# Other step durations for the list scheduler of an attention and two feed-forward layers

## The chip, the cores and the metric

The kernel runs on one core of a Trainium2 chip, in a single launch. The metric is the device time of that core in microseconds (us). Before the change it is 1063.86 us, the median of three runs.

## The reference

Four batches of eight heads, 576 positions, head size 64, go through a causal softmax attention that is mixed with a linear "memory" read; the result is a matrix of 2304 tokens by 512, which passes two feed-forward layers with 2048 hidden columns each.

```python
scores = scale * np.matmul(q, k.transpose(0, 1, 3, 2))        # causal mask, softmax -> a
local = np.matmul(a, v)
q_p = phi(q)                                                  # phi(x) = x + 1 for x > 0, exp(x) otherwise
mem_out = einsum('bhsd,bhde->bhse', q_p, M_prev) / (einsum('bhsd,bhd->bhs', q_p, z_prev) + 1e-06)
attn = g * mem_out + (1 - g) * local                          # g: one gate for each head
x = attn as (2304, 512)
r = np.maximum(x @ w_in1, 0); y = (s * r * r + b) @ w_out1    # first layer
h = y @ w_in2; out = (h * tanh(softplus(h))) @ w_out2         # second layer
```

All of it is float32. The feed-forward products are kept exact enough by splitting each operand into a high and a low part and adding three products.

## The kernel before

**An order made at build time.** Every operation is entered with `add(engine, us, prio, f, reads, writes)` as a step: an engine (PE, ACT, DVE, POOL, or the DMA queue that SyncE issues), a duration in microseconds that the program believes, and a rank. `Plan.order` then plays all steps through on a model of the engines: whenever an engine of the model is free, it takes the step of lowest rank among those whose inputs the model has ready and whose buffers (the `Ring`s, with few slots each) are free. The order in which the model starts the steps is the order in which the instructions are written into each engine's queue. On the chip each engine works its queue strictly in that order, and waits at its head where an input is late. So a duration written in `add` costs no time itself; it only decides what comes ahead of what. The model also has a TensorE clock of two levels (`pe_end`).

**Ranks.** Attention comes in units, one for a batch and a head. The eight of batch 0 are cut in two halves (ranks `PRE_A + STEP_A*h` and `PRE_B + STEP_B*h`); the 24 of batches 1 to 3 have `UNIT0 + UNIT*i`, that is 84.65, 106.78, 128.91 and so on. The first layer's weights are converted in 32 pieces of 128 x 512 (`convert`), whose ranks grow by `CONV` (3.0, 3.81, 4.18, 3.12 for a piece of the four groups), from 0 to 109.8. The first layer's products rank from 206 up by 5.53 a step, behind everything they compete with on TensorE; their elementwise work has the rank -1, ahead of everything.

**A unit of attention.** POOL, ACT and DVE make phi of q (`ex`); `norm_phi` (L423 to L426) forms the dot of each row of phi with z, one instruction for a tile of 128 rows, with its sum into `nm`; two small DVE steps make the gated reciprocal. For each tile, PE makes scores, DVE masks them and takes the largest (L476), POOL writes phi times the reciprocal into the same tile (`Pt`, L488: "phi's product"), and ACT takes the exponential (L485). The rows are then scaled, transposed by PE (L531), evicted by ACT and DVE, multiplied by M and v (L559), and written to `x_d`.

**A piece of weights.** The weights come as 8-byte words and are made into float32 by six instructions: a DMA (L620) into `raw` (two slots, with four more of borrowed room early on), two on ACT (L627 and L632), two on DVE (L634 and L635), one on POOL (L637). For the first layer ACT then rounds to the high part (L644) and DVE takes the low part (L646). The intermediate `w` has two slots (`w32=2`). For the second layer the piece goes to DRAM instead (L649), and comes back later.

**The first layer.** For 16 blocks of hidden columns (`fc`), `mm_in` (L698) makes h by 12 matmuls, ACT and DVE square the positive part and split it (L741, L742, L744, L745), and `y_part` (L758) adds 12 more matmuls to the accumulators `accs[j]`, which lie in the PSUM banks y0 and y1 for the first blocks of tokens. Columns `fc` 12 to 15 need the last group of weight pieces.

**Fillers.** While the model's time is between 7 and 85 us, the model sees PE idle, and it has done little in this tick of the model's clock, it puts in `zero_product` (L932 to L935): a matmul of zeros of 256 columns into the tile `idle`, which takes the place of bank y1. It computes nothing that is used.

Of the kernel before, what the change touches and what calls it, by code (L numbers as in the profile page):

```python
# [13 lines left out]
U32 = mybir.dt.uint32  # L14
AF = mybir.ActivationFunctionType
ALU = mybir.AluOpType
# [6 lines left out]
SIGN = -0x80000000  # L23
PE, ACT, DVE, POOL, DMA = range(5)
# [93 lines left out]
class Plan:  # L118
# [29 lines left out]
    def add(self, engine, us, prio, f, r=(), w=(), after=(), keep=(), share=1.0):  # L148


        bufs = list({id(b): b for b in (*r, *w, *keep) if b.ring is not None}.values())
        new = [b for b in bufs if b.maker is None]
        waits = {id(s): s for b in r for s in b.writers}
        waits.update((id(s), s) for s in after)
        s = Step(engine, us, prio, f, list(waits.values()), bufs, new)
        s.share = share
        s.left = len(waits)
        for x in waits.values():
            x.next.append(s)
        for b in bufs:  # L160
            b.users += 1
            if b.maker is None:
                b.maker = s
            elif id(b.maker) not in waits:
                b.maker.next_start.append(s)
                s.left += 1
        for b in w:
            b.writers.append(s)
        self.steps.append(s)
        return s  # L170
# [100 lines left out]
def attention_then_two_ffn(ctx: ExitStack, tc: tile.TileContext, qk, qz, vm, beta,  # L271
# [3 lines left out]
    nc = tc.nc  # L275
    B, H = qk.shape[:2]
    NQ, D = qz.shape[3] - 1, qz.shape[4]
# [20 lines left out]
    add = plan.add  # L298
# [66 lines left out]
    def unit(b, h, prio, groups=(TA, TB), place=None):  # L365
# [4 lines left out]
        def add(engine, us, f, r=(), w=(), keep=(), share=1.0):  # L370
            attention_steps.append(plan.add(engine, us, prio, f, r, w, keep=keep, share=share))
# [8 lines left out]
        else:  # L380
            qk_b, qn_b, vx_b = Buf(R["qk"], [P, SP + S]), Buf(R["qn"], [P, (NQ + 1) * D]), Buf(R["vx"], [P, NQ * D])
# [5 lines left out]
        def qkt(a, n):  # L387

            return qk_b.t[:, a - q0_:a - q0_ + n]

        def kt(a, n):
            return qk_b.t[:, k0_ + a:k0_ + a + n]
# [22 lines left out]
        ex = Buf(R["ex"], [P, NQ, D])  # L415
        nm = Buf(R["nm"], [P, 16])
        lo_t, n_t = tiles[0], len(tiles)
# [10 lines left out]
        def norm_gate():  # L428
# [3 lines left out]
        add(ACT, act_us(n_t * D), lambda: nc.scalar.activation(ex.t[:, mine], ex.t[:, mine], AF.Exp), [ex], [ex])  # L432
        add(DVE, dve_us(n_t * D), lambda: nc.vector.scalar_tensor_tensor(ex.t[:, mine], q_rows(), 0.0, ex.t[:, mine],
                                                                         op0=ALU.max, op1=ALU.add), [ex, qn_b], [ex])
        add(DVE, 0.22 * n_t, norm_phi, [ex, qn_b], [nm, qn_b])
        add(DVE, 0.13, norm_gate, [nm], [nm])
        add(DVE, 0.09, lambda: nc.vector.reciprocal(nm.t[:, mine], nm.t[:, mine]), [nm], [nm])  # L437

# [1 line left out]
        if not early:  # L440
# [4 lines left out]
                                                                    op=ALU.subtract), [qk_b, A], [A])  # L445
            add(DVE, dve_us(nkc), lambda: nc.vector.tensor_tensor(B2.t[:, :nkc], kt(0, nkc), B1.t[:, :nkc].bitcast(F32),
                                                                    op=ALU.subtract), [qk_b, B1], [B2])
# [8 lines left out]
        Pt = {t: Buf(R[ring[t]], [P, size[t]]) for t in tiles}  # L456
# [3 lines left out]
        def score(t):  # L460
            w = D + P * t
            for i, (lo, hi) in enumerate([(0, w)] if w <= 512 else [(0, w // 2 + 32), (w // 2 + 32, w)]):
                ps = Buf(R["a"], [P, 512])

                def mm(lo=lo, hi=hi, ps=ps):
                    if early:
                        nc.tensor.matmul(ps.t[:, :hi - lo], qkt(t * P, P)[:D], kt(lo, hi - lo)[:D],  # L467
                                         start=True, stop=True)
                    else:
                        lhs = A.t[:, t * P - q0_:(t + 1) * P - q0_]  # L470
                        nc.tensor.matmul(ps.t[:, :hi - lo], lhs, B1.t[:, lo:hi], start=True, stop=False)
                        nc.tensor.matmul(ps.t[:, :hi - lo], lhs, B2.t[:, lo:hi], start=False, stop=True)

                def least(lo=lo, hi=hi, ps=ps, i=i):

                    nc.vector.tensor_tensor_reduce(Pt[t].t[:, D + lo:D + hi], ps.t[:, :hi - lo],  # L476
                                                   mask[:, SP - w + lo:SP - w + hi], -SCALE,
                                                   mx.t[:, t:t + 1] if i else HUGE, ALU.add, ALU.min,
                                                   mx.t[:, t + i:t + i + 1])

                add(PE, (hi - lo) * 0.0017 if early else 0.07 + (hi - lo) * 0.0008, mm, score_in, [ps], [Pt[t], mx, rs], 0.5 if early else 1.0)
                add(DVE, 0.14 + 0.00105 * (hi - lo), least, [ps] + [mx_in[t]] * i, [Pt[t], mx_in[t]], [mx])

            def exp():
                nc.scalar.activation(Pt[t].t[:, D:w + D], Pt[t].t[:, D:w + D], AF.Exp, bias=mx.t[:, t + i:t + i + 1],  # L485
                                     scale=-1.0, accum_out=rs.t[:, t:t + 1])

            add(POOL, 0.3, lambda: nc.gpsimd.tensor_scalar(Pt[t].t[:, :D], ex.t[:, t, :], nm.t[:, t:t + 1], 1.0,  # L488
                                                           op0=ALU.mult, op1=ALU.mult), [ex, nm], [Pt[t]])
            add(ACT, 0.28 + 0.00083 * w, exp, [Pt[t], mx_in[t]], [Pt[t], rs_in[t]], [mx, rs])  # L490

# [114 lines left out]
    def convert(layer, prio, which, r, j, raw, after=()):  # L606


        w_in, w_out = ((w_in1, w_out1), (w_in2, w_out2))[layer - 1]
        fc = r * FPR + j  # L610
        src = w_in[j * P:(j + 1) * P, r * 512:(r + 1) * 512] if which == "in" else w_out[fc * P:(fc + 1) * P, :]
        w = Buf(R["w32"], [P, 512], I32)

        def words():
            return raw.t[:, :1024].rearrange("p (n two) -> p n two", two=2)

        def f32():
            return w.t.bitcast(F32)

        add(DMA, 1.5, prio, lambda: nc.sync.dma_start(words(), src.bitcast(I32).rearrange("p (n two) -> p n two", two=2)),  # L620
            w=[raw], after=after).lag = 1.0 if layer == 1 else 3.0

        e = on((C_W if layer == 1 else C2_W)[j])
        add(e, 0.52 if e == ACT else 0.335, prio,
            (lambda: nc.scalar.activation(f32(), words()[:, :, 1].bitcast(F32), AF.Copy, scale=2.0 ** -112)) if e == ACT else  # L627
            (lambda: nc.vector.tensor_scalar(f32(), words()[:, :, 1].bitcast(F32), 2.0 ** -112, None, op0=ALU.mult)),
            [raw], [w])

        low_words = Buf()
        add(ACT, 0.52, prio, lambda: nc.scalar.activation(words()[:, :, 0], words()[:, :, 0].bitcast(U32), AF.Copy,  # L632
                                                          scale=2.0 ** -29), [raw], [low_words])
        add(DVE, 0.335, prio, lambda: nc.vector.tensor_scalar(w.t, w.t, 3, None, op0=ALU.logical_shift_left), [w], [w])  # L634
        add(DVE, 0.6, prio, lambda: nc.vector.scalar_tensor_tensor(w.t, words()[:, :, 1], SIGN, w.t,  # L635
                                                                   op0=ALU.bitwise_and, op1=ALU.bitwise_or), [raw, w], [w])
        add(POOL, 1.23, prio, lambda: nc.gpsimd.tensor_tensor(w.t, w.t, words()[:, :, 0], op=ALU.add),  # L637
            [raw, low_words, w], [w])
        if layer == 1:
            hi, lo = W[1, f"w{which[0]}h", r], W[1, f"w{which[0]}l", r]  # L640
            hi_dve, lo_dve = C_HI[j] == "D", C_LO[j] == "D"
            half = Buf()
            add(DVE if hi_dve else ACT, 0.335 if hi_dve else 0.52, prio,
                lambda: (nc.vector.tensor_copy if hi_dve else nc.scalar.copy)(hi.t[:, j, :], f32()), [w], [hi, half])  # L644
            add(DVE if lo_dve else POOL, 0.6 if lo_dve else 1.23, prio,
                lambda: (nc.vector if lo_dve else nc.gpsimd).tensor_tensor(lo.t[:, j, :], f32(), hi.t[:, j, :].bitcast(F32),  # L646
                                                                           op=ALU.subtract), [w, half], [lo])
        else:
            add(DMA, 0.75, prio, lambda: nc.sync.dma_start(W2D[which, r][:, j, :], f32()), [w], [w2_in[which, r]]).lag = 1.5  # L649
# [239 lines left out]
    accs, halves = {}, {}  # L889
# [21 lines left out]
    for r in range(NR):  # L911
        for which in ("in", "out"):
            for j in (0, 2):
                split_second(-0.5, which, r, j)

    seq = [(blk, fc) for blk in range(NB2) for fc in range(NFC)]
    for i in range(len(seq) + LAG2):
        if i < len(seq):
# [11 lines left out]
    idle = []  # L930

    def zero_product():  # L932
        if not idle:
            idle.append(ps_y.tile([P, 512], F32, tag="y1_0", name="idle"))
        nc.tensor.matmul(idle[0][:, :256], mask[:, :P], mask[:, :256], start=True, stop=True)  # L935
# [46 lines left out]
```

## Time and profile before

| | us |
|---|---|
| median of 3 runs (1062.65 to 1064.59) | 1063.86 |
| the profiled execution's own time | 1059.81 |
| its span, from the first to the last instruction | 1058.0 |
| PE (matmuls) busy | 1027.7 |
| DVE busy | 665.0 |
| ACT busy | 533.4 |
| POOL busy | 218.5 |

The profile is of one execution. An engine is busy while one of its instructions runs; overlapping instructions count once. On DVE and ACT the record of an instruction overlaps the next one's by some hundredths of a microsecond, so the time that an instruction takes of its engine is read from its start to the next start, where the two follow without a gap. PE's clock is given as a share of its full speed: 1.00 is 2.4 GHz and 0.50 is 1.2 GHz.

### The profile page before, as it was taken

Reading aid. Unit: us, or ns where it says so; the run is one execution under the profiler, and the core shown is the slowest. Engines: PE = TensorE matmul, PEld = TensorE weight load, DVE = VectorE, ACT = ScalarE, POOL = GpSimd, SP = SyncE. Lnnn points to the kernel's source line nnn. Section 1 sums busy time; section 2 is a strip of 40 time slices with the busy share of each in tenths; the row PEclk is TensorE's granted clock in tenths of the full one; section 3 lists DMA queues with packets and bytes.
Section 4 is the critical chain, followed back from the end, with each engine's and each line's share of the span. In section 5 each row is a group of like instructions: output and inputs, shape, how many; then the busy total and the mean of one; then the engine's idle time right before and its main releaser. Section 6 shows DMA issues by size and latency. Waiting matters only on the chain. (4 is left out here: it accounts for less than half of the span.)

```text
span 1058.0 us, 17549 instructions
## 1 busy us (share of the span) xinstructions
PE 1027.7 (97%) x6011; PEld 891.4 (84%) x6011; DVE 665.0 (63%) x1962; ACT 533.4 (50%) x1267; POOL 218.5 (21%) x337
## 2 busy tenths in 40 slices
PE   7999997999999999999989999999999999999998
PEld 4567887999999999998768888888888888888887
DVE  7899999999999999955986666422312322222122
ACT  6887896888778888855445554312110211111111
POOL 6753443332333332212233300000000000000000
PEclk9999999999999999999999999999999999999999
DMA  9654562334322422257456764200200100010010
GB/s 274 186 168 141 174 182 76 105 112 144 95 87 80 134 87 87 71 176 212 136 169 200 241 205 155 86 1 1 80 1 1 35 26 0 1 40 1 1 41 20
DMA packets 52073, 106.66 MB, mean 101 GB/s; under 512 B 6672, under 2 KB 27664, under 8 KB 51984
## 3 DMA queue, kind: packets, MB, share of 16 engines
q1 hardware_dynamic: 51552, 105.54, 32.0%
q8 instruction: 47, 0.77, 0.3%
q14 instruction: 42, 0.34, 0.1%
q10 hardware_dynamic: 432, 0.01, 0.0%
HBM read 82.97 MB, written 22.54 MB: 100 GB/s over the span
## 5 line engine op out<-in xcount | busy, mean ns | idle before, releaser
L831 ACT ACTIVATE g<-h 128x512 f32<-128x512 f32 (+1 forms) x80 | 44.3, 554 | 313.8 <-PE h L698 292.1
L832 DVE CAST raw<-g 128x512 fp32r<-128x512 f32 (+1 forms) x60 | 24.0, 400 | 209.5 <-ACT g L831 162.1
L842 PE MATMUL o<-woh,raw 128*128 128x512 f32 x432 | 117.5, 390 | 0.0
L698 PE MATMUL h<-yh,wih 128*128 128x512 f32 (+1 forms) x448 | 113.3, 375 | 3.6 <-DVE g L742 3.6
L698 PE MATMUL h<-yh,wil 128*128 128x512 f32 (+1 forms) x448 | 112.9, 374 | 0.0
L698 PE MATMUL h<-yl,wih 128*128 128x512 f32 (+1 forms) x448 | 112.9, 374 | 0.0
L637 POOL TENSOR_TENSOR w<-w,raw 128x512 int32<-128x512 int32 x54 | 74.5, 1381 | 161.0 <-DVE w L635 109.6
L488 POOL TENSOR_SCALAR Pt<-ex,nm 128x64 f32<-128x64 f32 x148 | 73.6, 510 | 124.0 <-DVE nm L437 63.6
L698 PEld LDWEIGHTS h<-yh,wih 128*128 128x128 f32 x448 | 81.3, 188 | 21.1 <-DVE g L742 5.3
L698 PEld LDWEIGHTS h<-yh,wil 128*128 128x128 f32 x448 | 81.6, 188 | 16.1
L698 PEld LDWEIGHTS h<-yl,wih 128*128 128x128 f32 x448 | 81.6, 188 | 16.1
L842 PEld LDWEIGHTS o<-woh,raw 128*128 128x128 f32 x432 | 79.4, 188 | 14.9
L485 ACT ACTIVATE Pt<-Pt,mx 128x64 f32<-128x64 f32 (+4 forms) x148 | 81.6, 553 | 19.7 <-DVE mx L476 18.8
L531 PE MATMUL a<-ident,Pt 128*128 128x128 f32 x432 | 65.6, 279 | 6.9 <-POOL Pt L502 3.2
L539 DVE TENSOR_TENSOR PTl<-a,PTh 128x128 fp32r<-128x128 f32 (+1 forms) x144 | 63.8, 479 | 1.0 <-ACT PTh L536 0.4
L476 DVE CUSTOM_DVE_ANT_0 Pt<-a,mask 128x320 f32<-128x320 f32 (+3 forms) x148 | 59.6, 417 | 6.9 <-PE a L467 4.2
L531 PEld LDWEIGHTS a<-ident,Pt 128*128 128x128 f32 x432 | 49.8, 142 | 11.9 <-POOL Pt L502 5.5
L842 PE MATMUL o<-wol,raw 128*128 128x512 f32 x216 | 58.9, 390 | 0.0
L536 ACT CAST PTh<-a 128x128 fp32r<-128x128 f32 (+1 forms) x144 | 54.3, 434 | 5.7 <-PE a L531 4.8
L698 PE MATMUL h<-xh,wih 128*128 128x256 f32 x320 | 52.2, 288 | 2.7 <-DVE rt L742 2.6
L758 PE MATMUL y<-gh,wol 128*128 128x256 f32 x320 | 53.5, 290 | 0.0
L758 PE MATMUL y<-gl,woh 128*128 128x256 f32 x320 | 53.1, 288 | 0.0
(192 smaller groups left out, 2313.0 us busy)
## 6 DMA issues: line engine op xcount, KB each, us to landing
qk<-in_qk SPq DMA_DIRECT2D x24, 608.0 KB, 3.7
raw<-in_w_out SPq DMA_DIRECT2D x28, 512.0 KB, 4.3
raw<-in_w_in SPq DMA_DIRECT2D x26, 512.0 KB, 4.5
qn<-in_qz SPq DMA_DIRECT2D x29, 192.0 KB, 2.4
vx<-in_vm SPq DMA_DIRECT2D x29, 160.0 KB, 2.5
out<-ot SPq DMA_DIRECT2D x18, 256.0 KB, 2.2
w_in_d<-w SPq DMA_DIRECT2D x16, 256.0 KB, 3.1
w_out_d<-w SPq DMA_DIRECT2D x16, 256.0 KB, 3.3
```

Source lines behind the costliest of these rows:

```text
L476: nc.vector.tensor_tensor_reduce(Pt[t].t[:, D + lo:D + hi], ps.t[:, :hi - lo], mask[:, SP - w + lo:SP - w + hi], -SCALE, mx.t[:, t:t + 1] ...
L485: nc.scalar.activation(Pt[t].t[:, D:w + D], Pt[t].t[:, D:w + D], AF.Exp, bias=mx.t[:, t + i:t + i + 1], scale=-1.0, accum_out=rs.t[:, t:t ...
L488: add(POOL, 0.3, lambda: nc.gpsimd.tensor_scalar(Pt[t].t[:, :D], ex.t[:, t, :], nm.t[:, t:t + 1], 1.0, op0=ALU.mult, op1=ALU.mult), [ex, n ...
L531: nc.tensor.transpose(ps.t[:, c - c0, :], Pt[t].t[:, c * P:(c + 1) * P], ident)
L536: (nc.vector.tensor_copy if dve else nc.scalar.copy)(PT[0].t[:, at_], ps.t[:, :n])
L539: nc.vector.tensor_tensor(PT[1].t[:, at_], ps.t[:, :n], PT[0].t[:, at_].bitcast(F32), op=ALU.subtract)
L637: add(POOL, 1.23, prio, lambda: nc.gpsimd.tensor_tensor(w.t, w.t, words()[:, :, 0], op=ALU.add), [raw, low_words, w], [w])
L698: nc.tensor.matmul(ph, W[layer, nm, r].t[:, cc, o:o + P], x[:, cc], start=(part == 0 and cc == 0), stop=(part == 2 and cc == NCC - 1))
L758: nc.tensor.matmul(acc[ec // per].t[:, (ec % per) * n:(ec % per + 1) * n], W[1, nm, r].t[:, jj, ec * P:(ec + 1) * P], t(x), start=(fc == 0 ...
L831: add(ACT, act_us(n) + 0.06, ew, lambda: nc.scalar.activation(g.t, ph.t[:, :n], AF.Mish), [ph], [g])
L832: add(DVE, dve_us(n, True) + 0.08, ew, lambda: nc.vector.tensor_copy(gg.t[:, 0], g.t), [g], [gg, high])
L842: nc.tensor.matmul(acc[i].t, gg.t[:, k, i * P:(i + 1) * P], W[2, nm, r].t[:, jj, :], start=(fc == 0 and part == 0), stop=(fc == NFC - 1 an ...
```

## The change

Only durations that the scheduler believes are changed, and one guard is added. No instruction's operands change.

- phi's dot with z: 0.155 us for a tile where it was 0.22 (DVE).
- phi's product: 0.4 where it was 0.3 (POOL).
- a piece of weights: ACT 0.57 where it was 0.52, twice; DVE's shift 0.36 where it was 0.335; POOL's sum 1.29 where it was 1.23. For the first layer alone, DVE's three steps get another 0.2 each (`held`): the shift is 0.56, the bitwise step 0.8 where it was 0.6, the low part 0.8 where it was 0.6.
- `zero_product` puts in nothing once the accumulator of the first block of tokens in bank y1 (`accs[0][1]`) has been made; the model still counts its time.

```diff
-        add(DVE, 0.22 * n_t, norm_phi, [ex, qn_b], [nm, qn_b])
+        add(DVE, 0.155 * n_t, norm_phi, [ex, qn_b], [nm, qn_b])
...
-            add(POOL, 0.3, lambda: nc.gpsimd.tensor_scalar(Pt[t].t[:, :D], ex.t[:, t, :], nm.t[:, t:t + 1], 1.0,
+            add(POOL, 0.4, lambda: nc.gpsimd.tensor_scalar(Pt[t].t[:, :D], ex.t[:, t, :], nm.t[:, t:t + 1], 1.0,
...
-        add(e, 0.52 if e == ACT else 0.335, prio,
+        add(e, 0.57 if e == ACT else 0.335, prio,
...
-        add(ACT, 0.52, prio, lambda: nc.scalar.activation(words()[:, :, 0], words()[:, :, 0].bitcast(U32), AF.Copy,
+        add(ACT, 0.57, prio, lambda: nc.scalar.activation(words()[:, :, 0], words()[:, :, 0].bitcast(U32), AF.Copy,
...
-        add(DVE, 0.335, prio, lambda: nc.vector.tensor_scalar(w.t, w.t, 3, None, op0=ALU.logical_shift_left), [w], [w])
-        add(DVE, 0.6, prio, lambda: nc.vector.scalar_tensor_tensor(w.t, words()[:, :, 1], SIGN, w.t,
+        held = 0.2 if layer == 1 else 0.0
+        add(DVE, 0.36 + held, prio, lambda: nc.vector.tensor_scalar(w.t, w.t, 3, None, op0=ALU.logical_shift_left), [w], [w])
+        add(DVE, 0.6 + held, prio, lambda: nc.vector.scalar_tensor_tensor(w.t, words()[:, :, 1], SIGN, w.t,
...
-        add(POOL, 1.23, prio, lambda: nc.gpsimd.tensor_tensor(w.t, w.t, words()[:, :, 0], op=ALU.add),
+        add(POOL, 1.29, prio, lambda: nc.gpsimd.tensor_tensor(w.t, w.t, words()[:, :, 0], op=ALU.add),
...
-            add(DVE if lo_dve else POOL, 0.6 if lo_dve else 1.23, prio,
+            add(DVE if lo_dve else POOL, 0.6 + held if lo_dve else 1.23, prio,
...
+    y_first = accs[0]
...
     def zero_product():
+        if y_first[1].t is not None:
+            return
         if not idle:
```

## Rows read from the trace of the kernel before

**Rows 1.** The page: busy time of PE, and PE and DVE in 40 slices.
```profile
PE 1027.7 (97%) x6011; PEld 891.4 (84%) x6011; DVE 665.0 (63%) x1962; ACT 533.4 (50%) x1267; POOL 218.5 (21%) x337
PE   7999997999999999999989999999999999999998
DVE  7899999999999999955986666422312322222122
```
**Rows 2.** Stretches: their length, each engine's busy time (instructions), clock, DMA share, GB/s.
```profile
60.00:70.00 10.00, 7.53 (x39) 4.82 (x37) 8.45 (x25) 8.06 (x18) 6.49 (x7) 0.83 0.53 163
...
140.00:160.00 20.00, 18.19 (x142) 17.21 (x141) 19.84 (x49) 17.59 (x44) 9.99 (x10) 1.00 0.62 177
160.00:180.00 20.00, 15.11 (x101) 13.74 (x101) 18.53 (x68) 12.19 (x31) 7.04 (x13) 0.91 0.29 91
180.00:200.00 20.00, 20.00 (x169) 19.97 (x168) 19.49 (x70) 16.82 (x46) 6.54 (x13) 1.00 0.32 92
...
300.00:400.00 100.00, 99.87 (x816) 98.85 (x816) 95.42 (x379) 82.60 (x229) 31.66 (x64) 1.00 0.33 102
...
500.00:600.00 100.00, 95.31 (x413) 76.98 (x412) 77.54 (x122) 48.82 (x83) 30.55 (x22) 1.00 0.60 188
```
**Rows 3.** Waits from 140 to 182: engine, line, releaser: us in total, times, longest.
```profile
PE h L698 <- DVE rt L742: 2.2, 3, 0.9
PE a L471 <- DVE xs L570: 1.9, 1, 1.9
PE a L559 <- DVE PTl L539: 1.1, 2, 0.6
```
**Rows 4.** Lines over the span: duration ns min/median/max, first and last start, shape.
```profile
L425 DVE CUSTOM_DVE_ANT_0 qn<-ex,qn x136: 202/216/1283, 21.3 to 432.7; 128x64 f32<-128x64 f32 x136
L634 DVE TENSOR_SCALAR w<-w x64: 399/419/1574, 8.5 to 612.5; 128x512 int32<-128x512 int32 x64
L646 DVE TENSOR_TENSOR wol<-w,woh x16: 656/679/1772, 31.9 to 172.8; 128x512 fp32r<-128x512 f32 x16
L637 POOL TENSOR_TENSOR w<-w,raw x54: 1286/1312/1862, 9.9 to 613.9; 128x512 int32<-128x512 int32 x54
```
**Rows 5.** The order of time from 158 to 173: start, duration, engine, line.
```profile
158.42 0.66 ACT L627 ACTIVATE w<-raw 128x512 f32<-128x512 f32 x1
...
158.98 0.61 ACT L644 CAST woh<-w 128x512 fp32r<-128x512 f32 x1
...
161.78 0.68 DVE L635 SCALAR_TENSOR_TENSOR w<-raw,w 128x512 int32<-128x512 int32 x1
...
162.38 0.41 DVE L742 SCALAR_TENSOR_TENSOR rt<-h,rt 128x256 f32<-128x256 f32 x1
...
162.68 1.31 POOL L637 TENSOR_TENSOR w<-w,raw 128x512 int32<-128x512 int32 x1 [4.26 <-DVE w L635]
...
162.79 1.28 DVE L425 CUSTOM_DVE_ANT_0 qn<-ex,qn 128x64 f32<-128x64 f32 x1
...
164.01 0.22 DVE L425 CUSTOM_DVE_ANT_0 qn<-ex,qn 128x64 f32<-128x64 f32 x1
...
164.16 0.25 DVE L425 CUSTOM_DVE_ANT_0 qn<-ex,qn 128x64 f32<-128x64 f32 x1
...
170.60 1.85 POOL L488 TENSOR_SCALAR Pt<-ex,nm 128x64 f32<-128x64 f32 x5
...
172.47 0.66 PE L758 MATMUL y<-gh,woh 128*128 128x256 f32 x4
...
172.84 0.67 DVE L646 TENSOR_TENSOR wol<-w,woh 128x512 fp32r<-128x512 f32 x1
```
**Rows 6.** Two short stretches, columns as in rows 2.
```profile
164.00:168.00 4.00, 2.10 (x13) 1.37 (x12) 4.00 (x21) 2.91 (x6) 1.22 (x3) 1.00 0.19 49
168.00:172.00 4.00, 2.08 (x16) 1.73 (x16) 3.96 (x6) 2.55 (x6) 3.26 (x5) 1.00 0.00 0
```
**Rows 7.** The fillers: duration ns min/median/max, first and last start.
```profile
L935 PE MATMUL idle<-mask x121: 272/273/422, 8.8 to 72.7; 128*128 128x256 bf16 x121
```

## The prediction

> **What bounds the kernel now.** I read the page's 40 slices first [rows 1]: PE is busy in nine tenths or more of nearly every slice, 1027.7 us of a span of 1058.0, and DVE is nearly as full up to about 400 us and then falls off. So PE is the bound over most of the span, and what it loses it loses early. The stretches place the loss [rows 2]. From 180 on PE is full (20.00 of 20, then 99.87 of 100), and it stays so but for 4.69 us between 500 and 600. Ahead of 180 DVE is the fuller engine: 19.84 of 20 us from 140 to 160, and 18.53 of 20 from 160 to 180, while PE has 18.19 and 15.11. So up to 180 us DVE sets the pace, and after that PE does, at 1.00 of its clock. A change of order can bring time back only where PE is idle, slow, or at work that nobody uses.
>
> Those are these places. From 140 to 180 PE is idle for 1.81 + 4.89 = 6.70 us, and in the second half of that stretch the clock is 0.91, which is 0.09 x 20 = 1.8 us more: 8.5 us in all [rows 2]. From 60 to 70 it is idle for 2.47 us, with the clock at 0.83, another 1.7 us. Ahead of 72.7 us it runs 121 fillers [rows 7], which stand where it had nothing else to do.
>
> The waits between 140 and 182 say what PE stands for [rows 3]: 2.2 us for the first layer's square (three times, `rt`), 1.9 us for the eviction of an attention result, 1.1 us for a low part; these make 5.2 of the 6.7 us, and in each of them it is DVE that PE waits for. The worst stretch is 164 to 172, where PE works 2.10 + 2.08 = 4.18 of 8 us [rows 6]. It ends when the first layer's second product starts again at 172.47, and the last low part of the weights starts at 172.84 [rows 5]: columns 12 to 15 of the first block wait for the last pieces, and until those are there PE has only attention.
>
> **The change, part by part.** No instruction of the chip is added, removed or altered, except fillers that may be left out; the edit's direct cost is nothing. What it does is to shift the model's durations, and through them the order in the queues. So each edit is weighed by whether it brings the model nearer to the trace.
>
> ACT's two steps of a piece: 0.52 to 0.57. The trace has 158.98 - 158.42 = 0.56 us from start to start [rows 5], so the new value is right. POOL's sum: 1.23 to 1.29, against a least and median duration of 1.286 and 1.312 us [rows 4]; right. Phi's product: 0.3 to 0.4; five of them take 1.85 us, 0.37 each [rows 5]; nearer. The dot: 0.22 to 0.155; from start to start it is 164.16 - 164.01 = 0.15 us [rows 5], right for one that meets nothing, but another stood for 1.28 us beside a POOL sum of 1.31 us [rows 5].
>
> DVE's three steps of a piece are the large edit. The bitwise step takes 162.38 - 161.78 = 0.60 us from start to start, with a record of 0.68 [rows 5]. Taking the same overlap of 0.08 from the medians of the shift (419 ns) and the low part (679 ns) [rows 4] gives estimates of 0.34 and 0.60 us. These are the old values, 0.335, 0.6 and 0.6. The new ones, 0.56, 0.8 and 0.8, are 0.62 us a piece too long for a step that meets nothing. But the longest records of the same lines are 1.574 and 1.772 us [rows 4], so a part of them is held.
>
> What the model books up to the end of conversion therefore changes, for 32 pieces and 40 tiles of batch 0, by: DVE 32 x 0.625 - 40 x 0.065 = 20.0 - 2.6 = +17.4 us; ACT 32 x 0.10 = +3.2 us; POOL 32 x 0.06 + 40 x 0.1 = +5.9 us. Booked on conversion steps, it stands in for time that DVE loses on other steps too, such as the dot of 1.28 us. So the model's DVE gets fuller where the chip's DVE is full: its total comes nearer, its single steps don't.
>
> Where this bites is the queue of PE. Where the model believes that DVE is free sooner than it is, PE's queue has a product at its head whose input DVE still owes, with other products behind it that could run. Of the three waits for the square, 2.2 us, I take all as gone: a model whose DVE is 0.2 us later on each conversion step puts another PE step ahead of them. Of the other 4.5 us of idle and the 1.8 us of slow clock I take a third, 2.1 us, since they come from the last pieces being late, for which a fuller model only helps as far as it lets less of the later units slip in ahead. That is -4.3 us. The bounds are -8.5 us (all of that stretch comes back) and, the other way, the cost of a later last piece, below.
>
> The first stretch, up to 72.7 us, I cost at nothing: it is bounded by the first loads and by fillers, and its 2.47 us of idle and 1.7 us of slow clock can go either way by that amount. The second layer's pieces (ACT +0.1, DVE +0.025, POOL +0.06 us each) lie behind a PE that is full from 400 on, but for the 4.69 us from 500 to 600 [rows 2]; DVE has 22 us free of 100 there. I cost them at nothing, with 4.69 us as the most that could go and about 2 us as what a reshuffle may add.
>
> The guard takes away only what would have been a filler after the accumulator is made. In the kernel before, the last filler starts at 72.7, and the first layer's products follow it. If the new order has such places, PE is idle there instead. The trace has one idle spell of that kind, between 60 and 70, with the clock at 0.83 in that stretch [rows 2]: 1.7 us for each such spell, or nothing if there is none. I take nothing, because after 72.7 PE has real products, and keep 1.7 us for the range.
>
> Which step DVE loses to POOL, the trace shows directly: a dot that starts 0.11 us after POOL's sum ends with it, after 1.28 us [rows 5]. The Trainium skill (SBUF — State Buffer, "Who interferes with whom") says the pair of ports is an exclusive lock, and that the issue order decides who is blocked. The trace agrees. By that rule the hold belongs to whatever DVE starts after a POOL instruction, and a flat 0.2 us on conversion steps does not tell the scheduler where it falls; this speaks against the change, and its rival is the third below.
>
> The sum: 1059.81 - 4.3 = 1055.5 us for a profiled execution. The median of the runs before lies 4.05 us above the profiled one, and I carry this over: 1063.86 - 4.3 = 1059.6 us.
>
> **The rivals.** First, slower, by a later last piece. The model's conversion chain gets 0.785 us longer for each piece (0.10 on ACT, 0.625 on DVE, 0.06 on POOL), while the trace supports far less. With two slots for `w`, the model starts later pieces later, and other DVE work of later units, which ranks behind, slides in ahead of them in DVE's queue. On the chip this work then delays the last low part, now at 172.84. While PE waits for it, PE works 4.18 of 8 us, so each us of delay costs 0.48 us. If half of the 17.4 us that the model books more turns into delay, that is 8.7 x 0.48 = 4.2 us, and with another spell of slow clock (1.8 us) some 6 us: 1069.9 us. For it speaks that DVE's single steps are overbooked by 0.62 us a piece; against it, that a fuller DVE in the model has fewer free moments to give away. It decides from where the last low part starts later than about 177: 4.3 / 0.48 = 9 us of delay eats the whole forecast gain, and half of that leaves no difference to be measured.
>
> Second, no difference: DVE's work up to 180 is the same set of instructions, and DVE is nearly full; PE's loss only moves from one place to another. 1063.9 us, within 2.1 us. That the ranks decide nearly all of the order and the durations little, so that the change does next to nothing, comes to the same.
>
> Third, new holds: the new order puts other DVE steps behind POOL's sums. Each such hold costs up to 1.28 - 0.22 = 1.1 us of DVE; four more of them are 4.4 us, at 0.48 us of PE each 2.1 us, which leaves -2.2 us of the forecast: 1061.7 us; as many fewer would give 1057.5. This spreads the forecast rather than turning its sign.
>
> **How the numbers follow.** 0.2% is 2.1 us, about what a measurement of this kernel can tell from no change. The forecast (1055.4 to 1061.7, between all of the stretch's 8.5 us and the third rival's remainder) gets 0.46, the third rival's weaker half included; no difference 0.22; the slower rival 0.32, with times of 1066 to 1070. The predicted time is the forecast's, 1059.6 us. Cases of both signs hold most of the chance, so its own range is 1055.4 to 1061.7; the range for 8 in 10 runs from 1054 (the whole 8.5 us and a little of the stretch ahead) to 1070.
>
> **What would show it.** Right: from 140 to 180 PE idles for about 2 to 4 us less, waits for the square in PE's list shrink, the last low part starts no later than 172, and PE is full from some us before 178. Wrong: the last low part starts after 177, with PE at half of its time until then; or the clock is at 0.50 in a spell between 60 and 100 where fillers are left out; or the gain or loss comes from 500 to 600, where I booked nothing. The prediction is wrong in its reason if the time falls because of fewer fillers or an earlier start of the first layer, ahead of 100 us, and not at the end of conversion.

## The result and the profile after

The changed kernel is slower: 1068.2 us, the median of five runs (1068.01 to 1069.09), beside 1063.86 us; the ratio is 1.0052, with a 95% interval of 1.0039 to 1.0064. Of the two profiled executions the one after took 1069.09 us (span 1067.3) and the one before 1059.81 (span 1058.0). So the two traces lie 9.3 us apart where the medians lie 4.3 apart and the ratio says 5.5; the part above that is the luck of the two executions.

The page after (busy time, then PE, DVE and PE's clock in 40 slices; of before in [rows 1]):

```profile
PE 1034.0 (97%) x5997; PEld 894.0 (84%) x5997; DVE 664.8 (62%) x1962; ACT 534.0 (50%) x1267; POOL 219.0 (21%) x337
PE   7999978999999999999999999999999999999998
DVE  6889788999999999956896556422322322222122
PEclk9989889999999999999999999999999999999999
```

DVE, ACT and POOL are busy as long as before, to within 0.6 us. PE has 14 matmuls fewer, all of them fillers (107 where there were 121), and is yet busy for 6.3 us more, as part of its work ran at a lower clock. The loss lies early, where PE's slices and its clock dip. One stretch of the kernel before that [rows 2] leave out, then those of the kernel after, columns as in [rows 2]:

```profile
120.00:140.00 20.00, 19.66 (x141) 17.12 (x140) 18.87 (x69) 16.67 (x43) 7.54 (x11) 1.00 0.62 199
```
```profile
120.00:140.00 20.00, 17.97 (x95) 12.81 (x94) 16.11 (x58) 14.22 (x34) 5.84 (x8) 0.83 0.45 146
140.00:160.00 20.00, 14.28 (x83) 12.39 (x82) 17.94 (x54) 16.49 (x39) 9.91 (x12) 0.83 0.57 187
160.00:180.00 20.00, 15.63 (x116) 14.17 (x115) 18.54 (x49) 15.44 (x39) 8.51 (x12) 1.00 0.30 100
180.00:200.00 20.00, 19.48 (x149) 19.46 (x150) 18.41 (x75) 14.62 (x41) 6.18 (x14) 0.91 0.32 94
...
300.00:400.00 100.00, 99.61 (x817) 98.50 (x816) 96.07 (x383) 82.05 (x227) 32.85 (x64) 1.00 0.35 104
...
500.00:600.00 100.00, 96.51 (x422) 78.34 (x421) 79.86 (x125) 48.76 (x86) 29.97 (x21) 1.00 0.59 182
```

From 140 to 180 PE now idles 5.72 + 4.37 = 10.1 us, where it was 6.7 [rows 2]. From 120 to 160 its clock is at 0.83, where it was 1.00, and from 120 to 140 it idles 2.0 us, where it was 0.3. From about 188 on it is full, as it was from 178. What PE waits for from 140 to 190 has changed as well (columns as in [rows 3]):

```profile
PE a L531 <- POOL Pt L502: 3.3, 1, 3.3
PE a L531 <- DVE Pt L504: 2.0, 1, 2.0
PE h L699 <- DVE rt L743: 1.9, 3, 1.0
PE a L559 <- ACT PTl L536: 1.4, 1, 1.4
```

The waits for the square are nearly what they were (1.9 us, three, after 2.2); ahead of them stand waits for scaled rows of the attention. The lines are shifted by one from L635 on. The low part of the weights (duration ns min/median/max, first and last start) ends with one that starts at 181.5, where it was 172.8:

```profile
L647 DVE TENSOR_TENSOR wol<-w,woh x16: 666/681/1778, 41.0 to 181.5; 128x512 fp32r<-128x512 f32 x16
```

The view that tells most turned out to be a plain one: how far DVE has come after 220 us. First the kernel before, then the changed one (length; busy and instructions of PE, PEld, DVE, ACT, POOL; clock; DMA; GB/s):

```profile
0.00:220.00 220.00, 198.26 (x1296) 161.34 (x1297) 199.58 (x696) 175.59 (x453) 105.25 (x164) 0.98 0.53 161
```
```profile
0.00:220.00 220.00, 195.34 (x1203) 154.56 (x1204) 189.80 (x653) 168.87 (x429) 98.49 (x155) 0.95 0.50 157
```

DVE has done 653 instructions where it had done 696, and has been idle for 30.2 us where it was 20.4. That is 9.8 us more, the size of the distance between the two spans (9.3). What PE has yet to do after 220 us, its busy time over the span less that in this stretch, was 1027.7 - 198.3 = 829.4 us and is 1034.0 - 195.3 = 838.7 us. These 9.3 us are the whole distance between the spans, so the loss has happened by 220 us. The longest of DVE's waits in the changed kernel over this stretch are for ACT and PE:

```profile
DVE wol L647 <- ACT woh L645: 4.2, 2, 2.7
...
DVE w L635 <- ACT w L627: 3.9, 6, 1.0
DVE rs L507 <- ACT B L485: 2.8, 3, 1.3
DVE PTl L536 <- PE a L531: 2.5, 3, 1.4
```

One of them can be followed in the order of time of the changed kernel (start, duration, engine, line, in brackets the idle time ahead of it and who ended it):

```profile
129.69 3.63 PE L559 MATMUL a<-PTl,woh 128*64 128x256 f32 x10
...
130.89 0.68 DVE L636 SCALAR_TENSOR_TENSOR w<-raw,w 128x512 int32<-128x512 int32 x1
131.80 1.28 POOL L638 TENSOR_TENSOR w<-w,raw 128x512 int32<-128x512 int32 x1 [2.16 <-DVE w L636]
...
133.37 0.36 ACT L567 COPY xs<-a 64x256 f32<-64x256 f32 x1 [2.21 <-PE a L559]
133.63 0.62 ACT L645 CAST woh<-w 128x512 fp32r<-128x512 f32 x1
...
134.28 0.69 DVE L647 TENSOR_TENSOR wol<-w,woh 128x512 fp32r<-128x512 f32 x1 [2.72 <-ACT woh L645]
```

DVE's queue has nothing between the bitwise step of one piece (L636) and a low part (L647) that must wait for POOL's sum and ACT's rounding, so it stands still for 2.72 us. Most of this is the piece's own chain: POOL's sum takes 1.28 us and ACT's rounding 0.62. ACT's rounding is also queued behind an eviction that waits 2.21 us for PE, whose products ran at the lower clock (from 128 to 132 it is 0.50); as POOL's sum ends at 133.08 and the rounding starts at 133.63, this holds the piece up by 0.55 us at most.

### The profile page after: what moved, and what is told of

It reads as the page before. It is cut to its first block, busy times and chain, and to the rows that moved or that the text cites. A ratio compares the mean times of both kernels' runs of the same rounds, so it can differ in the third digit from the quotient of the medians.

```text
span 1067.3 us, 17502 instructions
## 1 busy us (share of the span) xinstructions
PE 1034.0 (97%) x5997; PEld 894.0 (84%) x5997; DVE 664.8 (62%) x1962; ACT 534.0 (50%) x1267; POOL 219.0 (21%) x337
## 4 chain that ended last, share of the span: by engine, by line
PE 83%; DVE 9%; ACT 2%; issue 2%; DMA 2%; POOL 1%; SPq 0%; DVEq 0%; ACTq 0%; POOLq 0%
PE h L699 33%; PE o L843 18%; PE y L759 11%; PE a L559 6%; PE a L531 4%; PE o L759 4%; PE a L467 2%; PE a L471 2%; PE a L472 2%; DVE total L673 1%; DVE w L636 1%; PE idle L939 1%; DVE PTl L539 1%; DVE Pt L476 1%; DMA wih<-in_qk 1%
## 5 line engine op out<-in xcount | busy, mean ns | idle before, releaser
L699 PE MATMUL h<-xl,wih 128*128 128x256 f32 x320 | 53.5, 290 | 0.0
```

Of the source, the lines that this page charges most:

```text
L699: nc.tensor.matmul(ph, W[layer, nm, r].t[:, cc, o:o + P], x[:, cc], start=(part == 0 and cc == 0), stop=(part == 2 and cc == NCC - 1))
```

## The experiments

Four theories were open. **A**: the overbooked DVE steps let the last weight piece slip back, and PE starves until it is there. **B**: an order fits its durations, and any shuffle costs something. **C**: the loss comes from the other durations. **D**, formed after the first eight runs: steps booked too long leave DVE without work on the chip, and since DVE sets the pace up to about 185 us, what it loses comes out at the end. Each ratio is with the kernel before on the same chip in the same session; the brackets are 95% intervals. The kernels of e1, e3, e4 and e11 also carry the guard of the change; it left nothing out in them, as the list that the scheduler makes and the trace hold the same number of fillers (124, 117, 126 and 137).

### The large edit alone, and the rest alone

e1, the extra on DVE's three steps, and of the rest of the change only the guard:

```diff
-        add(DVE, 0.335, prio, lambda: nc.vector.tensor_scalar(w.t, w.t, 3, ...
-        add(DVE, 0.6, prio, lambda: nc.vector.scalar_tensor_tensor(w.t, words()[:, :, 1], SIGN, ...
+        held = 0.2 if layer == 1 else 0.0
+        add(DVE, 0.335 + held, prio, lambda: nc.vector.tensor_scalar(w.t, w.t, 3, ...
+        add(DVE, 0.6 + held, prio, lambda: nc.vector.scalar_tensor_tensor(w.t, words()[:, :, 1], SIGN, ...
...
-            add(DVE if lo_dve else POOL, 0.6 if lo_dve else 1.23, prio,
+            add(DVE if lo_dve else POOL, 0.6 + held if lo_dve else 1.23, prio,
```

> The kernel before with one part of the change alone: the three DVE steps of a first-layer piece are booked 0.2 us longer (0.535, 0.8, 0.8). Theory A (the overbooked DVE steps let the last weight piece slip back, and PE starves until it is there): the last low part starts about 180 instead of 172.8, and the time is that of the changed kernel within 2 us, 1066 to 1070. Theory B (any shuffle of an order that fits its durations costs some us): 1066 to 1070 as well, but then the two runs with a change of 0.001 us show it too. Theory C (the loss comes from the other durations, phi's product and the ACT steps): 1062 to 1066, with the last low part at 171 to 175.

Measured: 1065.39 us, ratio 1.0046 (1.0028 to 1.0064). The last low part starts at 173.6. So with the large edit alone nearly the whole loss is there, but not by a late last piece: theory A's loss came without A's mark. DVE has done 680 instructions by 220 us:

```profile
0.00:220.00 220.00, 194.24 (x1261) 157.21 (x1262) 197.56 (x680) 173.47 (x442) 104.68 (x160) 0.98 0.54 161
```

e2, all of the change but that extra (0.01 stands for none):

```diff
-        held = 0.2 if layer == 1 else 0.0
+        held = 0.01 if layer == 1 else 0.0
```

> The changed kernel with 0.01 instead of 0.2 for the extra on DVE's three steps of a first-layer piece; all else of the change is in. Theory A: the last low part starts at 171 to 175 and the time comes back to 1062 to 1066. Theory C: it stays at 1066 to 1070. Theory B: anywhere from 1062 to 1070.

Measured: 1063.96 us, ratio 1.0028 (1.0015 to 1.0041), the last low part at 175.1. About half of the loss is there without the large edit. A's mark is missing in e1 and C's loss in e2; B, which allows nearly any time, is left, and the two runs below show that single orders can't divide the loss between the edits.

### A thousandth of a microsecond

e3 and e4 move one duration of the kernel before by 0.001 us (and carry the guard, without effect):

```diff
-        add(DVE, 0.6, prio, lambda: nc.vector.scalar_tensor_tensor(w.t, words()[:, :, 1], SIGN, w.t,
+        add(DVE, 0.601, prio, lambda: nc.vector.scalar_tensor_tensor(w.t, words()[:, :, 1], SIGN, w.t,
```

> The kernel before with one duration moved by a thousandth: DVE's bitwise step of a piece is booked 0.601 us instead of 0.6. Theory A: no cause for a loss, 1062 to 1066. Theory B: the order differs though the durations hardly do, so the time moves by 2 us or more, most likely up, 1066 to 1069.

```diff
-        add(DVE, 0.22 * n_t, norm_phi, [ex, qn_b], [nm, qn_b])
+        add(DVE, 0.219 * n_t, norm_phi, [ex, qn_b], [nm, qn_b])
```

> The kernel before with another duration moved by a thousandth: the dot is booked 0.219 us a tile instead of 0.22. As the run before it: theory A 1062 to 1066, theory B a move of 2 us or more. If the two moves differ in sign, the order has a scatter of its own, and no single time of a changed order tells of its cause without the trace.

Measured: e3 1070.28 us, ratio 1.0086 (1.0068 to 1.0104); e4 1060.83 us, ratio 0.9994 (0.9982 to 1.0005). So B holds in part: one thousandth reorders the queues enough to cost more than the whole change did, another does nothing. A time of one order is a draw from a spread of that size. The last low part of e3 starts at 181.9, as late as in the changed kernel. A part of its loss lies late, where PE's wait for the square of the last blocks of the first layer is 7.4 us over the span; before it was 3.6:

```profile
PE h L698 <- DVE g L742: 7.4, 6, 3.7
```

### The clock, and the last piece

e5 and e6 leave the order as it is and put products of zeros where the scheduler's model left PE idle after 85 us, 154 in the changed kernel and 55 in the one before:

```diff
+                if end > 85.0 and s.start > end + 0.25:
+                    for _ in range(int((s.start - end) / 0.107) + 2):
+                        self.zeros()
...
+    def zeros():
+        if open_y[0] is not None:
+            nc.tensor.matmul(open_y[0].t[:, :256], mask[:, :P], mask[:, :256], start=False, stop=False)
```

> The changed kernel in the same order, with 154 more products of zeros on TensorE, added to an open accumulator, wherever the scheduler's own model left PE idle after 85 us (ahead of 13 or so late attention steps). They can't shorten a wait; they only keep the engine at work in it. If the slow clock carries most of what the change costs (the profiles: 12.0 us at a reduced clock share against 3.6 before, idle 24.7 against 21.7), the clock in the spells at 120 to 160 and 180 to 200 stays at 1.00 and the time falls by 2 to 5 us against the changed kernel, to a ratio of 1.000 to 1.003 with the kernel before. If the idle time itself carries it, the ratio stays at 1.004 to 1.007.

> The kernel before in its own order, with 55 such products of zeros in the places where its model left PE idle. Where the slow clock matters it gains too, but less, as its profile has only one spell of it after 100 us (1.8 us): ratio 0.997 to 1.000. If the zeros only cost, 1.000 to 1.003.

Measured: e5 1071.15 us, ratio 1.0084 (1.0067 to 1.0101); e6 1061.89 us, ratio 1.0001 (0.9989 to 1.0013). The clock of the profiled execution rose from 0.989 to 0.995 in e5, and from 120 to 200 PE is busy as never before:

```profile
120.00:160.00 40.00, 38.52 (x276) 32.70 (x276) 36.40 (x116) 32.02 (x75) 18.73 (x22) 0.96 0.53 176
160.00:200.00 40.00, 39.71 (x328) 38.08 (x327) 36.48 (x124) 29.83 (x80) 13.84 (x24) 1.00 0.32 98
```

DVE is idle for 3.6 and 3.5 us in these two stretches, where it was 6.0 and 3.1 without the zeros, and has done 657 instructions by 220 us, as against 653. So with most of the clock back, DVE came hardly further and the time is no better. That the clock carries none of the loss is not shown: the 154 zeros take 18.7 us of PE themselves, and what they cost where real work arrives meanwhile this run does not separate. In the kernel before, 55 of them, 7.0 us of PE, cost nothing that can be measured.

e7 ranks the last pieces ahead in the changed kernel, and e8 ranks them behind in the kernel before:

```diff
-CONV = (3.0, 3.81, 4.18, 3.12)
+CONV = (3.0, 3.81, 3.2, 1.0)
```

> The changed kernel with the last two groups of weight pieces ranked ahead of the later attention units (steps of rank 3.2 and 1.0 where they are 4.18 and 3.12); all its new durations stay. The order up to the first product of the first layer is nearly the same. If the late last piece carries the loss, the last low part starts some 8 us earlier than 181.5, at 172 to 176, and the ratio falls to 0.999 to 1.003. If the new durations cost in another way, the ratio stays at 1.004 or more with the piece early.

```diff
-CONV = (3.0, 3.81, 4.18, 3.12)
+CONV = (3.0, 3.81, 4.18, 7.0)
```

> The kernel before with its old durations, and the last group of pieces ranked 7.0 apart instead of 3.12, so that later attention work goes ahead of them. If the late last piece carries the loss, the last low part starts at 179 to 183 and the ratio is 1.003 to 1.007, like the changed kernel's, without any of its durations. If not, 0.998 to 1.002.

Measured: e7 1073.94 us, ratio 1.0106 (1.0089 to 1.0124); e8 1063.42 us, ratio 1.0011 (1.0000 to 1.0023). The low part's line, first in e7, then in e8:

```profile
L647 DVE TENSOR_TENSOR wol<-w,woh x16: 667/679/1770, 40.9 to 178.6; 128x512 fp32r<-128x512 f32 x16
```
```profile
L646 DVE TENSOR_TENSOR wol<-w,woh x16: 654/680/1779, 32.2 to 181.9; 128x512 fp32r<-128x512 f32 x16
```

In e8 the last piece is as late as in the changed kernel, 181.9 against 181.5, and costs a fifth of what the change does; in e7 it is 3 us earlier, not the 8 that were expected, and the time is worse. Theory A falls, mainly by e8: a late last piece goes along with most of the losses here, but does not make them by itself. What is alike in e8 and the kernel before is DVE's progress, 693 instructions against 696:

```profile
0.00:220.00 220.00, 197.39 (x1258) 159.48 (x1259) 198.36 (x693) 175.22 (x452) 104.41 (x163) 0.97 0.54 161
```

DVE did attention work instead of the last pieces, and as it stays over 95% busy until 400 us [rows 2], that work was not lost.

### How much is booked, and on what

e9 and e10 take another extra, e11 books too much on another DVE step, e12 takes work away from DVE in the order of before:

```diff
-        held = 0.2 if layer == 1 else 0.0
+        held = 0.1 if layer == 1 else 0.0
```

> The changed kernel with an extra of 0.1 instead of 0.2 us on DVE's three steps of a first-layer piece. Theory D (steps booked too long leave DVE without work on the chip: the model puts the next step behind a time that the chip doesn't need, and its input isn't there yet; the lost DVE time then shows at the end, since DVE sets the pace up to about 185 us): DVE idle from 60 to 220 lies between 7.0 (extra 0.01) and 17.7 us (extra 0.2), near 12, and the ratio near 1.002 to 1.005. Theory B (any shuffle has its own scatter, and the size of the extra has no bearing): DVE idle and ratio anywhere, 0.998 to 1.009.

```diff
-        held = 0.2 if layer == 1 else 0.0
+        held = 0.3 if layer == 1 else 0.0
```

> The changed kernel with an extra of 0.3 us. Theory D: DVE idle from 60 to 220 above 18 us, near 22, and a ratio of 1.008 to 1.014. Theory B: no more idle than with 0.2, and a ratio of 0.998 to 1.009.

```diff
-                add(DVE, 0.14 + 0.00105 * (hi - lo), least, ...
+                add(DVE, 0.14 + 0.00105 * (hi - lo) + (0.4 if early else 0.0), least, ...
```

> The kernel before with its own durations for the pieces, and 0.4 us too much booked on another kind of DVE step: the mask and maximum of the scores of batch 0, 48 steps, 19.2 us in all as the change books on the pieces. Theory D: the same loss from another place, DVE idle from 60 to 220 near 17 us and a ratio of 1.004 to 1.010. If only the pieces' chain matters (a late last piece): 0.998 to 1.003.

```diff
-        add(DVE, 0.6, prio, lambda: nc.vector.scalar_tensor_tensor(w.t, words()[:, :, 1], SIGN, w.t,
+        cols = 256 if layer == 1 else 512
+        add(DVE, 0.6, prio, lambda: nc.vector.scalar_tensor_tensor(w.t[:, :cols], words()[:, :cols, 1], SIGN, w.t[:, :cols],
```

> The kernel before in its own order, with the bitwise step of the 32 first-layer pieces done on half of its columns, so that DVE has about 32 x 0.27 = 8.6 us less to do ahead of 175 us; the weights' signs are then wrong in the other half. If DVE sets the pace up to about 185 us, and time that it loses or gains there comes out at the end, the time falls by 5 to 8 us, a ratio of 0.992 to 0.996. If PE or the loads set it, the ratio is 0.998 to 1.001.

Measured: e9 1058.64 us, ratio 0.9970 (0.9957 to 0.9983); e10 1075.26 us, ratio 1.0130 (1.0113 to 1.0146); e11 1068.91 us, ratio 1.0061 (1.0047 to 1.0074); e12 1054.72 us, ratio 0.9932 (0.9919 to 0.9945). The first 220 us of the four, in this order:

```profile
0.00:220.00 220.00, 197.80 (x1288) 159.92 (x1289) 200.35 (x696) 176.13 (x453) 104.81 (x163) 0.98 0.53 161
```
```profile
0.00:220.00 220.00, 192.70 (x1199) 152.89 (x1200) 190.53 (x645) 167.81 (x424) 100.11 (x155) 0.95 0.51 156
```
```profile
0.00:220.00 220.00, 196.19 (x1283) 158.69 (x1284) 197.34 (x679) 172.43 (x442) 101.15 (x160) 0.98 0.52 160
```
```profile
0.00:220.00 220.00, 201.85 (x1348) 165.72 (x1349) 196.74 (x725) 180.69 (x469) 103.92 (x168) 1.00 0.54 165
```

e12 shows who sets the pace: about 8.6 us less work on DVE gives 0.0068 x 1062.3 = 7.2 us less time, with the same order. The shorter step also shortens the chain of each piece (the last low part starts at 168.0 instead of 172.8), which this run does not separate; by e8, the last piece alone is worth little. In e11 as much booked on another DVE step goes with as large a loss, so the pieces need not be special; as one order of so wide a spread, it proves no more. Theory D's mark, DVE idle from 60 to 220, came out too small: 8.8 us in e9 (near 12 expected, and a ratio of 1.002 to 1.005), 18.3 in e10 (near 22) and 9.3 in e11 (near 17). In e11 it is the count, 679, that falls, not the busy time alone.

### The neighbours

Since e3 had shown so large a scatter, four neighbours of 0.1 and 0.2 were run, each with the same one-line edit (`held` 0.09, 0.15, 0.18, 0.22):

> The changed kernel with an extra of 0.09 us. If the size of the extra decides, the ratio is within 0.002 of the run with 0.1 (0.997), that is 0.995 to 0.999. If an order's own scatter is as large as what the nudge by a thousandth showed (+0.0086), it may be anywhere from 0.996 to 1.009, and the gain with 0.1 was a draw.

> The changed kernel with an extra of 0.15 us. Size decides: between the runs with 0.1 (0.997) and 0.2 (1.005), near 1.001. Scatter: anywhere from 0.996 to 1.009.

> The changed kernel with an extra of 0.18 us. Size decides: 1.003 to 1.007, DVE idle from 60 to 220 at 14 us or more. Scatter: 0.998 to 1.012.

> The changed kernel with an extra of 0.22 us. Size decides: 1.004 to 1.010, DVE idle from 60 to 220 at 16 us or more. Scatter: 0.998 to 1.012.

Measured: e13 1065.67 us, ratio 1.0028 (1.0017 to 1.0039); e14 1064.3 us, 1.0019 (1.0009 to 1.0029); e15 1071.06 us, 1.0079 (1.0064 to 1.0095); e16 1070.88 us, 1.0084 (1.0068 to 1.0099). By their expectations, e13 speaks for scatter (0.995 to 0.999 if size decides), e14 for size, e15 lies just above the range for size, and e16 in it. The four extras up to 0.15 lie between 0.9970 and 1.0028, and the four from 0.18 on between 1.0052 and 1.0130, without overlap; that the four largest extras are the four slowest has a chance of 1 in 70 by scatter alone. So the size seems to shift the level, while the orders scatter over 0.6% within the lower and 0.8% within the upper four; and e3, with no extra at all, lies at 1.0086. No single order shows what an extra costs. The gain of e9 is real for that one order and beats both kernels, but 0.09 loses 0.28%: it is a good draw, not a value that is right. DVE idle from 60 to 220 is 14.2 us in e15, but 11.6 in e16, where at least 16 were expected: the mark of theory D, idle time, is again too narrow.

What idle time leaves out can be read from the same traces. Some DVE records last far longer than others of the same operation and shape, as the dot of 1.28 us in [rows 5]. Take those of the first 220 us that exceed 1.25 times the median of their kind over all the traces, and add up what is above the median: 21.9 us in 35 records before, 22.0 in 33 in the changed kernel, 28.2 in 39 in e3. Every one of them, in all 18 traces, overlaps a POOL instruction. This is called held time below.

All runs, by DVE's instructions in the first 220 us:

| kernel | DVE instructions | DVE idle, us | DVE held, us | ratio |
|---|---|---|---|---|
| e12, less DVE work | 725 | 23.3 | 20.4 | 0.9932 |
| e4, dot 0.219 | 701 | 18.6 | 22.3 | 0.9994 |
| before | 696 | 20.4 | 21.9 | 1 |
| e9, extra 0.1 | 696 | 19.6 | 24.1 | 0.9970 |
| e6, before with zeros | 694 | 21.3 | 22.3 | 1.0001 |
| e8, late pieces | 693 | 21.6 | 22.2 | 1.0011 |
| e2, extra 0.01 | 691 | 18.6 | 25.1 | 1.0028 |
| e14, extra 0.15 | 680 | 21.6 | 25.2 | 1.0019 |
| e1, extra alone | 680 | 22.4 | 24.1 | 1.0046 |
| e11, scores overbooked | 679 | 22.7 | 25.0 | 1.0061 |
| e13, extra 0.09 | 678 | 23.4 | 23.7 | 1.0028 |
| e3, bitwise 0.601 | 678 | 19.5 | 28.2 | 1.0086 |
| e16, extra 0.22 | 658 | 24.1 | 27.7 | 1.0084 |
| e5, after with zeros | 657 | 28.4 | 23.0 | 1.0084 |
| e15, extra 0.18 | 654 | 26.6 | 25.0 | 1.0079 |
| after | 653 | 30.2 | 22.0 | 1.0052 |
| e7, early pieces | 649 | 29.7 | 24.9 | 1.0106 |
| e10, extra 0.3 | 645 | 29.5 | 24.8 | 1.0130 |

These are 18 kernels in 15 orders, as e5, e6 and e12 keep the order of after or before; e12 has less work besides. The count orders the ratios (rank correlation, in size, 0.92) better than the start of the last low part (0.72), the clock of this stretch (0.68) or idle time (0.59) do. Idle and held time together say why it falls. In the changed kernel idle time alone grows, by 9.8 us; in e3 held time, by 6.3 us, with 0.9 us less of idle time; in e10, e15 and e16 both.

## Why the prediction was wrong, step by step

- **Sign.** Forecast was 1059.6 us and faster; it is 1068.2 us and slower, inside the range of 1054 to 1070. The slower rival, with 0.32, had the right sign, and its 1069.9 us is near, for a reason that did not hold (below).
- **The step that failed** is the one from the durations to PE's queue. The working had in hand that DVE's three steps cost what they were booked at before, to a few hundredths [rows 4, 5], and that the extra overbooks them by 0.62 us a piece. It then let the model's total decide ("its total comes nearer"), and expected PE's head-of-queue waits to shrink. The gain of 4.3 us from 140 to 180, which rests on this step alone, came out as 3.4 us more of PE's idle time there. What the runs show in its place: DVE, which sets the pace there (e12), does less by 220 us, 653 instructions for 696, and in the changed kernel all of that is idle time, 9.8 us more of it, in which its queue has a step at its head whose input is late. That the extra does this is supported by the two levels of extras and by e11, and not proven, since e3 loses more without any extra. The working also had no term for the scatter of the orders themselves, which e3 puts at 0.86%, more than the whole change.
- **The waits for the square**, 2.2 us, were taken as gone; 1.9 us are left, and the waits for scaled rows are new. From 120 to 140, where nothing was booked, PE idles 1.7 us more, and its clock falls from 1.00 to 0.83.
- **The slower rival's mechanism** was right in its first half at most. It put the last low part 8.7 us later, and it is 8.7 us later (172.8 to 181.5); that the two figures agree is luck, as e1, with the same extra alone, has it at 173.6. The price, 0.48 us for each us of delay, is wrong: e8 has the same delay for 0.11%. It took DVE's earlier attention work as worth nothing, though DVE is 95% busy until 400 us.
- **New holds**, the third rival: held time is what it was, 22.0 us after 21.9, so they had no part in this change; e3 shows that an order can have them, 6.3 us more. The hold does not belong to whatever DVE starts after a POOL instruction: before, 257 of DVE's records up to 220 us start while a POOL instruction runs, and 35 are held.
- **The clock**: a term of 1.8 us for a spell was added to the time of the slower rival. With the spells nearly gone in e5 the time is no better, so that term was not shown to be worth anything. The one place where the order of time shows the clock reaching further is 129 to 134, through ACT's eviction to DVE, by 0.55 us at most.
- **Booked at nothing and right**: the guard left no filler out, as the list that the scheduler makes holds 107 and the trace has 107, the last at 75.5 and ahead of the first accumulation at 80.5; the first product of the first layer starts at 71.9, where it was 72.7; and from 500 to 600 PE idles 3.49 us instead of 4.69. From 60 to 80 the clock costs 1.6 us more (0.72 and 0.94 in the two halves, after 0.91 for the whole), about the 1.7 us that this stretch was given either way.
- **"No difference"** was argued from DVE being nearly full. DVE was full, but not so full that an order could not take another 10 us from it.

What stays open: how much of the loss the extra brings and how much is the draw of this one order, why a change of a thousandth (e3) puts more of DVE's steps where POOL holds them, and what the slow clock is worth without the zeros.

## What to carry to other kernels

Where an order is fixed at build time by believed durations, durations nearer to the trace are no promise of a faster order: those of e2 are all within some hundredths of a microsecond of what the trace shows from start to start, and it took 0.28% longer than the kernel before. A margin added to the steps of the engine that sets the pace is not on the safe side: the four largest extras here were all slower than the four smallest, and in the changed kernel the engine stood still for 9.8 us more. Count how many instructions the pacing engine has done at a fixed time; this sorted the 18 kernels better than idle time, the clock or the last piece of a chain did. Then split what is missing into idle time and instructions that last longer than others of their kind. And run neighbours of a value before believing it, since an order may move by 0.9% on a thousandth of a microsecond.

## What the runs showed of the hardware

PE kept at work by products of zeros had its clock back (0.989 to 0.995 over the span, 0.83 to 0.96 from 120 to 160), and the kernel was not faster for it (ratio 1.0084 after 1.0052). The zeros took 18.7 us of PE; what they cost and what the clock gave are not separated.

All of DVE's records of the first 220 us that lasted more than 1.25 times the median of their kind overlapped a POOL instruction, in every one of the 18 traces; in the kernel before they are 35 records with 21.9 us above the median. Most records that start beside POOL are not held: 35 of 257 are.
